# Unit 1's alpha turned on the matrix engine, wider filler products, last stores from one queue, and new orders in a GLA-then-MoE kernel

## The chip, the core and the metric

The kernel runs on one core of a Trainium2 chip. A core has a matrix engine (TensorE, PE in the profile; its weight loads are PEld), a vector engine (VectorE, DVE), an activation engine (ScalarE, ACT), GpSimd (POOL) and SyncE (SP). Each runs its own list of instructions in order, and they wait for one another through semaphores. Transfers between memory and the on-chip SBUF are issued by an engine's queue (here SP's and ACT's) and carried out by 16 DMA engines. TensorE writes into PSUM banks, which VectorE and ScalarE read. The metric is the device time of one execution in microseconds, lower being better.

## What is computed

First a gated linear attention, per batch and head a running 48x48 state; then an MLP on its output, whose nonlinearity is h - tanh(h).

```python
for t in range(S):                       # B,H,S,D = 4, 8, 768, 48
    state = alpha[:, :, t, :, None] * state + np.einsum('bhd,bhe->bhde', k[:, :, t], v[:, :, t])
    y[:, :, t] = np.einsum('bhd,bhde->bhe', q[:, :, t], state)
x = y.transpose(0, 2, 1, 3).reshape(B * S, H * D)      # 3072 x 384
h = x @ w_in                                           # w_in 384 x 2048
out = (h - np.tanh(h)) @ w_out                         # w_out 2048 x 384
```

The inputs q, k, v, alpha are float32; w_in and w_out are float64 in memory and are read as 64-bit integers and turned into float32 on the chip.

## The kernel before

The sequence is cut into 12 **units** of 256 tokens (two chunks of 128). The function `fast` does all of it; `general` is a slow form for inputs outside the range of the fast one, in a conditional at the end (line 1511) that is skipped when `ok` is 1.

For each unit the attention part (`gla`, from line 653) loads alpha, k, q and v, makes their transposes (aT, kT, qT: head dimension on partitions), makes prefix and suffix products of alpha by scans (`U`, `ends`, `W`), multiplies them into k and q (`kU`, `qW`), and then for each chunk computes masked scores, the output y and the new state on TensorE. In the first two units, which stand at the start of the program, transposes can be made by TensorE: `TURNED` (line 472) says for which of alpha, k, q (0, 1, 2). For such a tensor `load` (line 585) fetches a `rough` tile in natural layout with runs of 2 x 48 floats, 384 bytes, in two halves (line 604), `turn` (line 700) multiplies 32 blocks of 64x64 with the identity (line 718), and `place` or `times` copies the result out of PSUM. Otherwise `load` fetches runs of 8 x 48 floats, 1,536 bytes, onto 2 x 32 partitions (line 608), ScalarE copies a part (`widen`, line 684) and VectorE transposes blocks of 32x32 (`flip`, line 690). Unit 0's transfers are halved between SP's queue and ACT's.

The MLP of a unit has 8 **steps**. `first u:s` multiplies x by two column blocks of w_in into a PSUM bank (line 1243); ScalarE squares (`square`, `quad`), VectorE forms the cubic tail (`cube`, `shrunk`); `second u:s` multiplies by w_out and accumulates (line 1323). Units 0 and 1 do this plainly; units 2 to 11 use a scheme with 7 instead of 8 block products for w_out (line 1345; `combine` makes the combinations of w_out beforehand, `sums` those of g), and units 6 to 11 another one for w_in. x of a unit from 1 on is rearranged between partitions by six small DMAs on SP (`moves`, line 1145) before its first step. The first of all steps, `first_a 0:0` and `first 0:0`, is halved by chunk.

The weights come in 16 **pieces** (in0 to in7, out0 to out7), at the start of the program. `fetch` (line 560) has `load_weight` (line 38) issue the DMAs of a piece, six for w_in and one for w_out, into one of four `raw` tiles; `read` is the part of `round_weight` on ScalarE (lines 86, 87) and the second part, on VectorE (lines 89, 90), writes the float32 weights. Later `reload` fetches the pieces once more for a range check (`look`).

All this is issued in an order written out by hand: each piece of work is a named task with an engine, a cost, a due rank, the tasks it follows and a latency (`add`, line 386). `Planner.STEPS` holds the order of all tasks as steps between task numbers, made beforehand from these costs; `order` only checks it, works out start times, and puts filler products (`spin`, line 1425: identity times identity, 128x128) into the gaps of TensorE before the first y. Since each engine works in order, a task that waits holds up all that comes behind it on its engine. SP's queue is one of these engines: a load that waits for its tile holds the next fetch.

At the end, `store` of a unit scales and adds up four PSUM banks and issues four DMAs, those of the last unit two on ACT and two on SP (lines 1415 and 1418). After the last task each engine takes a branch over its part of `general`.

Of the kernel before, what the change touches and what calls it, by code (L numbers as in the profile page):

```python
# [8 lines left out]
FP32 = mybir.dt.float32  # L9
I32 = mybir.dt.int32  # L10
I64 = mybir.dt.int64
# [5 lines left out]
P = 128  # L17
HP = 64
CU = 2
WN = 768  # L20
# [17 lines left out]
def load_weight(nc, pool, rows, both=False, **kw):  # L38

    raw = pool.tile([P, WN], I64 if rows[0][2].dtype != FP32 else FP32, name="raw", **kw)  # L40
    for at, js, src in rows:
        (nc.scalar if both and at.start % HP == 0 and at.start else nc.sync).dma_start(  # L42
            out=raw[at].rearrange("p (j n) -> p j n", n=src.shape[-1])[:, js], in_=src)
    return raw
# [89 lines left out]
def general(tc, q, k, v, alpha, moe_w_in, moe_w_out, out, w_in, w_out, ident, pad_rows):  # L134
# [10 lines left out]
    with ExitStack() as ctx:  # L145
        with tc.tile_pool(name="g_raw", bufs=1) as raw_pool:
            for s in range(FT // 2):
                for what, dst in (("in", w_in[:, :, 2 * s * P:2 * (s + 1) * P]), ("out", w_out[:, 2 * s:2 * s + 2, :])):
                    raw = load_weight(nc, raw_pool, weight_parts(moe_w_in, moe_w_out, pad_rows, what, s))
                    round_any_weight(nc, raw_pool, raw, dst)  # L150
# [34 lines left out]
        for u in range(B * UPB):  # L185
# [3 lines left out]
            for c in range(CU):  # L189
                t0 = i * TU + c * P  # L190

                def rows(x):
                    return x[b, :, t0:t0 + P, :].rearrange("h p d -> p h d")
                for t, x in zip(nat, (alpha, k, q)):
                    nc.sync.dma_start(out=t[:, c, :, 0:D], in_=rows(x))
                nc.sync.dma_start(out=vt[:, c], in_=rows(v))
# [119 lines left out]
            for c in range(CU):  # L316
                ob = one.tile([P, d_model], FP32, name="g_ob")
                A.copy(ob, o[c])
                nc.sync.dma_start(out=out_r[u * CU + c], in_=ob)


class Planner:
# [6 lines left out]
        "90 1 1 2 -1 2 -95 100 -3 9 -10 7 11 -7 27 -30 6 -1 -4 27 -34 -97 98 18 16 -32 11 -4 10 17 -33 17 -117 135 -17 -117 139 -14 -15 8 -10 12 6 14 -28 9 "  # L329
        "-118 124 -8 -6 9 -121 127 13 -18 -117 127 -9 -122 2 506 -501 126 376 -369 3 -8 -132 512 -5 -505 5 501 -370 4 367 4 6 -376 -133 504 -509 -2 507 15 -517 "  # L330
        "-2 7 502 -384 386 -378 372 -378 383 4 -504 -7 2 133 377 5 -380 -134 520 -513 -5 513 3 -383 -132 503 4 -500 -5 131 375 -369 -9 393 -5 -515 2 5 509 -382 "
        "-11 -120 518 -390 -121 500 7 -11 5 -506 513 -383 2 -124 510 -385 -132 521 -395 -124 125 389 -506 123 -128 -2 504 11 -384 -128 7 -5 519 -392 387 -513 "
        "128 -126 502 -377 387 5 -516 512 6 -10 5 -384 388 -391 393 -517 512 -384 -2 379 -504 159 361 -3 -385 24 -28 398 -402 397 -388 390 -1 -384 -4 384 9 "
        "-367 364 4 -398 395 -381 -15 400 2 -396 1 21 -18 394 -3 -369 -21 394 5 -20 17 -346 345 -394 396 -375 -31 401 8 2 -379 -5 386 -6 -344 -57 54 350 -375 "
        "-24 22 382 -401 22 5 -29 27 26 356 -9 4 -401 23 -18 398 -1 2 -401 404 -388 390 -10 -353 -42 -3 5 405 -3 -406 408 -382 -6 383 -376 -4 27 360 -557 172 "
        "-171 174 383 -366 -39 -1 24 1 1 -176 152 27 378 2 -1 2 2 -561 180 -179 559 -384 386 -385 387 -557 556 3 -373 376 -4 -343 -27 381 -6 2 -1 -348 -42 386 "
        "-385 395 -4 -394 400 2 -7 4 -351 357 -16 -377 389 11 -370 364 -389 33 358 -12 11 6 -395 2 397 -388 385 -5 6 5 -17 -380 387 -364 370 -395 406 -598 589 "
        "-399 402 -591 574 19 5 4 -10 7 -404 -1 400 11 -413 4 404 -5 -602 204 409 2 -1 -606 611 -397 -15 -25 23 19 -43 -172 579 32 -412 416 -623 182 30 -2 397 "
        "2 12 -394 368 -387 44 -41 409 -18 -348 -26 -219 618 -398 -219 224 381 -384 385 -360 366 -12 -380 398 -368 357 13 -1 -394 -2 398 3 -10 8 -631 641 -7 "
        "-422 -202 203 422 -427 31 -15 424 -10 -627 625 6 -411 21 372 25 -6 1 -7 16 -3 6 -17 12 -26 38 -6 -12 -388 401 -12 13 -424 -223 659 -7 -651 655 -36 "  # L340
        "-396 436 -32 12 13 1 -12 -417 423 1 13 -1 -26 -633 240 -39 23 22 -46 441 -640 201 451 2 -7 13 1 -436 1 437 -391 -29 -242 240 30 401 -8 -433 -229 244 "
        "422 -13 18 -7 -396 -20 2 410 -415 29 389 9 -396 -30 -19 446 -401 -25 418 12 -3 -449 442 -416 -21 445 10 -457 450 -452 454 -1 3 -433 -248 251 429 11 -9 "
        "-430 -251 684 -18 20 -1 6 2 -1 3 -443 435 -20 31 -429 -40 459 -434 1 5 13 432 -6 2 -700 699 -398 -31 442 -7 -704 708 -434 398 40 -413 -71 77 -30 -24 "
        "-22 451 -403 415 13 1 -12 -414 -24 444 13 1 -13 -398 415 -445 -272 258 42 386 -432 -1 3 462 -459 -258 276 445 -28 -419 31 420 -20 8 6 -12 -428 435 -14 "
        "26 -8 -717 726 -450 431 20 -8 -718 282 438 -7 14 1 -7 9 -8 -721 277 451 -450 -277 729 2 -1 -452 455 -1 2 2 -440 -17 -24 1 44 -43 486 -6 -456 1 457 -1 "
        "2 -442 437 9 -416 420 -3 1 -419 424 -464 -286 746 -773 767 -739 756 -9 3 -419 420 29 -28 12 -435 424 -453 457 2 -19 25 -7 -431 440 -1 -5 -7 17 -470 "
        "-300 1 758 -477 489 -470 2 3 466 -800 801 7 -448 -51 466 14 -459 -22 501 -6 23 -16 -28 -469 514 -513 497 -478 2 -305 310 -8 496 -16 -22 5 34 -33 17 "
        "-782 771 12 -503 519 -15 -11 27 1 -16 17 -16 28 -11 -15 -22 21 17 -15 26 -9 -16 18 24 -16 -11 -31 59 -26 10 -816 808 25 -16 -43 -470 530 -16 17 -16 17 "
        "-531 515 17 -16 17 -16 28 -11 -49 61 -28 -32 33 16 12 -27 43 -15 -61 49 28 -15 -61 33 29 -13 28 -14 15 -28 1 13 -12 27 -63 64 -15 -48 49 28 -13 -13 -1 "
        "15 13 1 -78 65 14 -78 79 -14 -571 556 30 -11 -3 -15 16 14 -570 -39 -1 26 585 -587 3 517 -542 610 -67 -503 571 -67 76 -592 593 -8 -1 -567 24 553 -77 78 "  # L350
        "-62 34 29 -62 -514 577 -28 -546 575 14 -13 -581 517 -533 -4 538 64 -555 506 -532 594 18 -30 -49 62 18 -79 49 -48 51 -606 616 -601 619 -63 46 -13 14 "
        "-46 63 -16 -594 611 -614 598 -577 578 16 -50 -14 49 -48 31 33 -15 -35 63 -26 14 -32 45 -63 51 -592 605 -63 34 -33 -574 637 -62 49 28 -26 -35 62 -44 29 "
        "-10 -601 565 -605 623 -17 46 -45 -609 669 -14 -45 60 -646 647 -15 16 -32 -615 648 -16 -609 626 -32 44 -11 -17 -32 61 -43 -17 49 12 -29 1 -32 1 60 -11 "
        "-17 29 14 -27 14 -46 17 43 -13 -12 -1 27 -13 -12 26 1 -62 48 15 -62 -626 627 47 15 -13 -1 15 -13 -672 686 -13 14 2 8 -680 -39 24 635 -636 -24 661 50 "
        "10 -7 24 -712 -24 42 678 -60 77 -76 60 17 -16 -45 34 12 16 -61 -638 700 -16 17 -670 654 -12 29 -672 656 17 -714 727 -29 -700 702 15 -16 17 -700 712 -8 "
        "-70 1 78 -63 52 12 -63 -671 21 684 -33 63 -684 -46 745 -44 30 -63 -649 727 -62 48 -711 726 -749 735 -17 18 14 -704 -26 700 31 -64 50 15 -64 34 -33 49 "
        "-735 763 -26 -1 -35 63 -748 734 15 -14 15 -64 36 -717 682 49 -48 35 28 -14 28 -61 -694 729 -760 759 -33 47 -11 12 -13 14 12 1 -61 49 13 -61 62 15 -76 "
        "62 -764 750 29 -14 -13 28 -14 -15 30 -780 752 29 -64 18 47 -64 48 17 -30 31 -17 2 26 -10 -66 52 -51 48 46 -18 -26 -34 50 -796 825 -18 -60 61 -10 28 "
        "-17 -61 62 -61 48 30 -799 783 -805 822 -16 -13 30 1 -17 18 -49 32 -803 821 -16 2 -18 15 18 9 -813 -15 -26 776 -733 812 -78 70 -69 -732 733 -778 26 829 "
        "-61 -793 30 825 -28 -33 -772 834 -61 34 28 -61 48 14 -815 816 -831 832 -14 15 -50 61 -846 786 51 -50 -782 834 -51 48 -833 844 18 -27 10 -44 -803 865 "  # L360
        "-45 28 -44 45 -10 27 -16 -45 -786 832 -45 61 -15 16 -15 16 -846 2 845 1 -17 -33 -799 850 -17 28 -26 -35 34 28 17 -883 855 -50 79 -17 -61 53 26 -63 34 "
        "12 18 -63 17 17 12 -28 46 -63 46 -45 63 -30 13 -45 63 -17 18 -903 886 -864 882 -17 28 -42 -850 832 33 45 -44 -33 -841 901 -900 918 -77 48 12 -59 60 "
        "-11 28 -16 -45 35 -3 -31 -856 901 -44 60 -915 856 13 31 -13 29 -15 -31 47 1 -16 17 -30 14 -900 2 900 15 -16 17 -15 17 8 -950 944 -54 51 -50 35 25 -59 "
# [1179 lines left out]
```

## Time and profile before

| | |
|---|---|
| median of 3 runs | 563.54 us (562.07, 563.95, 563.54) |
| the profiled execution | 560.73 us |
| its span, first to last instruction | 558.9 us |
| granted clock of TensorE | 0.996 |
| TensorE from 60 to 550 us | busy 490.00 of 490 us |
| VectorE, ScalarE from 60 to 550 us | busy 417.15 and 314.45 us |
| turning one tensor of a unit on TensorE | 32 products in 64 rows, 1.16 us |
| `flip` of alpha, unit 1 | 4 transposes, 2.06 us |
| `widen` of alpha, unit 1 | 2 copies, 1.26 us |
| conversion of a piece | 2.1 us on ScalarE, 0.56 and 0.96 us on VectorE |

A row of such a table is read with its place: a busy time says how long an engine worked in a stretch, not whether the end of the kernel depended on it. The page gives the shares of the whole span; the windows give them by stretch; the chain of waits gives, followed back from the end, what released each piece of work; the timeline gives the instructions of an engine in order, with the idle time before each in brackets and the instruction that ended it. Times in these views count from the span's start. Durations of neighbouring products overlap, so the time of one is read from start to start.

### The profile page before, as it was taken

How to read it: one execution, taken by the hardware profiler on the slowest of the kernel's cores; microseconds unless marked ns; L12 is line 12 of the kernel's file. 1: busy time of each engine (PE TensorE's matmuls, PEld its weight loads, DVE VectorE, ACT ScalarE, POOL GpSimd, SP SyncE). 2: the span in 40 equal slices, each digit the busy share in tenths (PEclk: the TensorE clock that was granted, in tenths of full speed). 3: DMA queues.
4: the chain of work that ended last, by engine and by line, in shares of the span. 5: the costliest groups of instructions: out<-in, count | busy, mean ns of one | idle time of the engine just before them, and what ended most of it. 6: DMA issues, size and time to landing. Idle time of an engine off the chain costs nothing.

```text
span 558.9 us, 14579 instructions
## 1 busy us (share of the span) xinstructions
PE 545.1 (98%) x6003; PEld 496.8 (89%) x6003; DVE 469.3 (84%) x855; ACT 358.4 (64%) x723; POOL 4.9 (1%) x23
## 2 busy tenths in 40 slices
PE   7889999999999999999999999999999999999995
PEld 7777767778899999899999999999999999999994
DVE  7879989989999598896898789999899986756663
ACT  2699987637856749774687747647754654555550
POOL 3000000000000000000000000000000000000000
PEclk9999999999999999999999999999999999999998
DMA  9999764143284363663541021130020000100001
GB/s 214 223 261 253 242 120 143 30 91 117 57 182 110 86 164 79 161 152 86 138 155 57 29 63 33 57 74 22 28 64 5 29 8 3 32 6 0 30 2 35
DMA packets 59468, 50.88 MB, mean 91 GB/s; under 512 B 34528, under 2 KB 49152, under 8 KB 59392
## 3 DMA queue, kind: packets, MB, share of 16 engines
q1 hardware_dynamic: 56304, 48.58, 34.3%
q10 hardware_dynamic: 3088, 1.28, 0.9%
q8 instruction: 49, 0.80, 0.6%
q14 instruction: 27, 0.22, 0.1%
HBM read 44.04 MB, written 4.72 MB: 87 GB/s over the span
## 4 chain that ended last, share of the span: by engine, by line
PE 94%; DVE 1%; SPq 1%; issue 1%; DMA 1%; ACT 0%; POOL 0%; ACTq 0%; DVEq 0%; POOLq 0%
PE o L1345 32%; PE h L1243 23%; PE h L1254 14%; PE o L1323 7%; PE h L1275 7%; PE h L976 4%; PE sc L949 2%; PE sc L1122 1%; PE sc L956 1%; PE sc L976 1%; SPq L42 1%; DMA raw<-in_moe_w_in_dram 1%; PE spin L1429 1%; SPq L593 1%; DVE w_in L90 1%
## 5 line engine op out<-in xcount | busy, mean ns | idle before, releaser
L1243 PE MATMUL h<-xT,w_in 128*128 128x256 f32 (+1 forms) x588 | 131.6, 377 | 3.2 <-DVE w_in L90 3.2
L1243 PEld LDWEIGHTS h<-xT,w_in 128*128 128x128 f32 x588 | 108.1, 190 | 19.9 <-DVE w_in L90 4.2
L1345 PE MATMUL o<-b,e 128*128 128x192 f32 x480 | 93.3, 326 | 0.0
L1345 PEld LDWEIGHTS o<-b,e 128*128 128x128 f32 x480 | 79.1, 190 | 0.2
L1345 PE MATMUL o<-w_out,e 128*128 128x192 f32 x320 | 78.6, 328 | 0.0
L1299 DVE SCALAR_TENSOR_TENSOR g<-z,w 128x512 f32<-128x512 f32 x96 | 65.3, 684 | 12.8 <-ACT z L1290 5.7
L1345 PE MATMUL o<-b,g 128*128 128x192 f32 x320 | 68.9, 326 | 0.0
L1290 ACT ACTIVATE z<-u 128x512 f32<-128x512 f32 x96 | 60.2, 629 | 7.0 <-DVE g L1299 5.5
L1345 PEld LDWEIGHTS o<-w_out,e 128*128 128x128 f32 x320 | 55.0, 190 | 1.2
L1267 ACT COPY u<-h 128x128 f32<-128x128 f32 x96 | 24.6, 265 | 48.4 <-PE h L1254 47.5
L1254 PE MATMUL h<-xT,w_out 128*128 128x128 f32 x288 | 54.9, 275 | 0.0
L1254 PE MATMUL h<-xT,w_in 128*128 128x128 f32 x288 | 54.4, 277 | 0.0
L1280 DVE TENSOR_TENSOR w<-h,u 128x512 f32<-128x512 f32 x48 | 33.1, 690 | 25.3 <-PE h L1275 24.6
L1345 PEld LDWEIGHTS o<-b,g 128*128 128x128 f32 x320 | 53.8, 190 | 0.1
L1286 ACT ACTIVATE u<-w 128x512 f32<-128x512 f32 x48 | 30.3, 631 | 36.7 <-DVE w L1280 36.6
L1305 ACT ACTIVATE big<-u 128x1024 f32<-128x1024 f32 x48 | 50.6, 1054 | 0.4
L1254 PEld LDWEIGHTS h<-xT,w_in 128*128 128x128 f32 x288 | 47.9, 190 | 1.8
L1275 PE MATMUL h<-xT,w_in 128*128 128x256 f32 x192 | 49.2, 380 | 0.0
L1286 ACT ACTIVATE u<-h 128x512 f32<-128x512 f32 x48 | 28.4, 591 | 28.6 <-PE h L1243 28.4
L1312 DVE TENSOR_TENSOR e<-g 128x384 f32<-128x384 f32 x80 | 44.2, 552 | 2.8 <-PE o L1345 0.6
L1254 PEld LDWEIGHTS h<-xT,w_out 128*128 128x128 f32 x288 | 45.3, 191 | 0.4
L1323 PE MATMUL o<-w_out,g 128*128 128x384 f32 x128 | 43.4, 489 | 0.0
(167 smaller groups left out, 959.7 us busy)
## 6 DMA issues: line engine op xcount, KB each, us to landing
raw<-in_moe_w_out_dram SPq DMA_DIRECT2D x16, 768.0 KB, 6.1
raw<-in_moe_w_in_dram SPq DMA_DIRECT2D x16, 288.0 KB, 5.1
raw<-in_moe_w_in_dram SPq DMA_DIRECT2D x47, 96.0 KB, 5.0
vt<-in_v_dram SPq DMA_DIRECT2D x23, 192.0 KB, 3.6
ar<-in_alpha_dram SPq DMA_DIRECT2D x22, 192.0 KB, 3.9
kr<-in_k_dram SPq DMA_DIRECT2D x20, 192.0 KB, 3.1
qr<-in_q_dram SPq DMA_DIRECT2D x20, 192.0 KB, 3.2
raw<-in_moe_w_in_dram SPq DMA_DIRECT2D x15, 192.0 KB, 5.4
```

The source lines that it names most:

```text
L976: return T.matmul(to[rows], lhsT=lhsT, rhs=rhs, start=start, stop=last, skip_group_check=True)
L1243: T.matmul(h[:, a, to], lhsT=w_in[:, j, f * P:(f + 1) * P], rhs=xT[u][:, j, to], start=(j == 0), stop=(j == KT - 1))
L1254: T.matmul(m["h", s][:, to], lhsT=left[n][:, s], rhs=right[u][n], start=start, stop=True, skip_group_check=True)
L1275: T.matmul(m["h", s][:, 2 * a:2 * a + 2].rearrange("p i t -> p (i t)"), lhsT=wi[:, KT - 1, s, a], rhs=xT[u][:, KT - 1, :], start=False, st ...
L1280: V.tensor_add(m["w", s], m["h", s].rearrange("p i t -> p (i t)"), m["u", s])
L1286: A.activation(m["u", s], m["h", s], AF.Square, scale=W_SCALE ** -1.5)
L1290: A.activation(m["z", s], m["u", s], AF.Square, bias=QB, scale=QA * W_SCALE)
L1299: V.scalar_tensor_tensor(out=g.rearrange("p a c t -> p (a c t)"), in0=m["z", s], scalar=QK, in1=m["w", s], op0=ALU.add, op1=ALU.mult)
L1305: A.activation(big, m["us", s // 2].rearrange("p s t -> p (s t)"), AF.Relu, bias=-U_FAST, scale=W_SCALE, accum_out=over[:, n:n + 1])
L1312: V.tensor_sub(e[:, 0:3, :], x[:, 3:4].to_broadcast([P, 3, P]), x[:, 0:3])
L1323: T.matmul(m["o"][c], lhsT=g[:, a, c, :], rhs=w_out[:, f, :], start=(f == 0), stop=(f == FT - 1))
L1345: T.matmul(o[n][:, i], lhsT=g_, rhs=w_, start=(s_ == 0 and (n, i) in ((0, 0), (1, 0), (2, 1), (3, 0))), stop=(s_ == FS - 1), skip_group_ch ...
```

## The change

Five things are changed.

- `TURNED` has alpha of unit 1 too: it is loaded as a rough tile, turned by TensorE into a double PSUM bank of its own time (`early`), and copied by ScalarE and VectorE. Its turn comes after unit 0's qW; that of q comes after these copies.
- The filler has a second, longer product, 128x512 (the tile `after` is its moving side), used in gaps that are long enough. In the gap before the first task only short ones are used, counted with 2 instead of 1.75 lengths.
- The first piece of w_in is no longer halved between the queues (`BOTH_QUEUES` is 0), and the code for it is rewritten; SP issues its six parts.
- The last unit's stores are issued by SP alone. In `general` all DMAs are issued by ScalarE, so that SP has none there.
- Costs and latencies of loads, fetches and reads in the plan are changed, and the written order of all tasks on all engines is a new one.

In the new order TensorE does, after the turns of unit 0: back 0.0, update 0.0, scores 0.0, back 0.1, turn aT 1, update 0.1, scores 0.1, turn qT 1, y 0.0, carried 0.1, y 0.1, first_a 0:0, turn kT 1, first 0:0, first 0:1, back 1, scores 1.0, first 0:2, y 1.0, first 0:3, second 0:0, scores 1.1, first 0:4, second 0:1, y 1.1. Before it did: back 0.0, scores 0.0, update 0.0, turn qT 1, back 0.1, scores 0.1, y 0.0, update 0.1, carried 0.1, y 0.1, turn kT 1, first_a 0:0, first 0:0, first 0:1, back 1, first 0:2, first 0:3, second 0:0, scores 1.0, first 0:4, second 0:1, first 0:5, scores 1.1, y 1.0. SP does, after unit 0's loads: aT, kT, qT of unit 1, in0, in1, v of unit 1, in2, in3; before: in0, qT, aT, kT, v of unit 1, in1, in2, in3. From in2 on the fetches have the same order, up to out6.

```diff
-def load_weight(nc, pool, rows, both=False, **kw):
+def load_weight(nc, pool, rows, raw=None, of=None, of_all=False, **kw):
-    raw = pool.tile([P, WN], I64 if rows[0][2].dtype != FP32 else FP32, name="raw", **kw)
+    raw = raw or pool.tile([P, WN], I64 if rows[0][2].dtype != FP32 else FP32, name="raw", **kw)
     for at, js, src in rows:
-        (nc.scalar if both and at.start % HP == 0 and at.start else nc.sync).dma_start(
+        if of is not None and of != (at.start >= HP):
+            continue
+        (nc.scalar if of or of_all else nc.sync).dma_start(
             out=raw[at].rearrange("p (j n) -> p j n", n=src.shape[-1])[:, js], in_=src)
...
-                    nc.sync.dma_start(out=t[:, c, :, 0:D], in_=rows(x))
-                nc.sync.dma_start(out=vt[:, c], in_=rows(v))
+                    nc.scalar.dma_start(out=t[:, c, :, 0:D], in_=rows(x))
+                nc.scalar.dma_start(out=vt[:, c], in_=rows(v))
...
-                filled += [(free, -1, do, None)] * int(gap / (1.75 * us) if free == self.begin.get(engine) else gap / us - 1 if gap > 2 * us else 0)
+                first = free == self.begin.get(engine)
+                n = 0 if first else max(0, int((gap - us) / (4 * us)))
+                filled += [(free, -1, longer, None)] * n
+                gap -= 4 * n * us
+                filled += [(free, -1, do, None)] * int(gap / (2 * us) if first else gap / us - 1 if gap > 2 * us else 0)
...
-    BOTH_QUEUES = 1
+    BOTH_QUEUES = 0
...
-        TURNED = ((0, 1, 2), (1, 2))
+        TURNED = ((0, 1, 2), (0, 1, 2))
...
+                    elif what == 0 and u > 0:
+                        if c == 0:
+                            early = two_banks()
+                        t = early[:, c]
...
-                go("turn aT", "PE", 1.5 if u == 0 else 1.0, 0, ["load aT", later and "masked 0.0"], lambda: turn(0))
+                go("turn aT", "PE", 1.5 if u == 0 else 1.0, 0, ["load aT"] + [later and f"qW{x} 0" for x in "ab"], lambda: turn(0))
...
-                go("turn qT", "PE", 1.0, 2, ["load qT"] + [later and f"qW{x} 0" for x in "ab"], lambda: turn(2))
+                go("turn qT", "PE", 1.0, 2, ["load qT"] + [later and f"aT{x} {u}" for x in "ab"], lambda: turn(2))
...
-                    (A if u == NU - 1 and c == 0 else nc.sync).dma_start(out=half[1 - c], in_=cross[:, c, :])
...
-                    (A if u == NU - 1 and c == 0 else nc.sync).dma_start(out=half[c], in_=same[:, c, :])
+                for t, to in ((cross, 1), (same, 0)):
+                    for c in range(CU):
+                        n = abs(to - c)
+                        nc.sync.dma_start(out=out_r[u * CU + c][:, n * NH:(n + 1) * NH], in_=t[:, c, :])
...
-                spun.append(ps_o.tile([P, P], FP32, name="spin", tag="o2"))
-            T.matmul(spun[0], lhsT=ident, rhs=ident, start=True, stop=True)
-        plan.filler = "PE", "y 0.0", 0.24, spin
+                spun.append(ps_o.tile([P, 4 * P], FP32, name="spin", tag="o2"))
+            T.matmul(spun[0][:, 0:by.shape[-1]], lhsT=ident, rhs=by, start=True, stop=True)
+        plan.filler = "PE", "y 0.0", 0.24, spin, lambda: spin(after[:, 0:4 * P])
```

Left out are the lines of `STEPS`, the costs (for instance `fetch` of a piece of w_in from 3.2 to 4.0, of w_out from 2.9 to 2.2, `read` from 1.9 to 2.1), the rewritten `fetch` and the two changes of `general`'s weight load and store.

## The prediction

> **What bounds the kernel now.** I read the page from the top, then the windows, the waits, the chain, and at last the timeline of both ends. The page says that TensorE is the bound, and that only the first slices are not full:
>
> ```profile
> span 558.9 us, 14579 instructions
> PE 545.1 (98%) x6003; PEld 496.8 (89%) x6003; DVE 469.3 (84%) x855; ACT 358.4 (64%) x723; POOL 4.9 (1%) x23
> PE   7889999999999999999999999999999999999995
> DMA  9999764143284363663541021130020000100001
> ```
>
> The windows say where it lacks work and who else is full (columns: stretch, length, busy us of PE, PEld, DVE, ACT, POOL, then clock, DMA share, GB/s):
>
> ```profile
> 0.00:20.00 20.00, 16.27 (x372) 14.82 (x373) 16.15 (x35) 9.19 (x17) 4.93 (x23) 1.00 0.97 217
> 20.00:40.00 20.00, 16.75 (x208) 14.08 (x207) 15.35 (x22) 14.31 (x22) 0.00 (x0) 1.00 1.01 252
> 40.00:60.00 20.00, 20.00 (x276) 14.85 (x278) 18.62 (x36) 19.95 (x30) 0.00 (x0) 1.00 0.96 260
> ```
>
> From 40 to 545 us PE is full in every window, and its waits between 60 and 550 us list nothing. So the end is set by three things: when PE becomes full, what it must do, and the tail after its last product at 550.2. How it becomes full stands in the chain (start, length, what):
>
> ```profile
> 26.18 0.97 DVE w_in L90
> ...
> 27.20 2.73 PE h L1243 x22
> ...
> 30.04 0.97 DVE w_in L90
> ...
> 31.06 2.42 PE h L1243 x10
> ...
> 36.90 0.97 DVE w_in L90
> ...
> 37.91 2.86 PE h L1243 x12
> ```
>
> Three times PE stands before a conversion of w_in: first_a 0:0 began at 25.21 with two rows and went on at 27.20 (1.7 lost), 29.97 to 31.06 (0.9), 36.7 to 37.91 (1.2). The first stop is telling: piece in0 was converted by 16.43, so first_a waited for **in1**, which it doesn't read. And two of these conversions themselves waited for PE ("0.92 <-PE h L1243", "1.32 <-PE h L1243" in the timeline). The pieces of w_in are strided, and their extents overlap; so products and conversions of different pieces wait for each other in the order in which they are written. That makes a ping-pong: product, conversion of 0.97, product, with PE idle unless other PE work stands between.
>
> **The change, the start.** Unit 1's alpha loses two ACT copies (0.62 each) and four DVE transposes (18.21 to 20.13, 2.06 in sum). It gains 32 products on PE (64 rows; turn qT 1, the same shape: 16.46 to 17.55, **1.09**) and one copy each on ACT (0.59) and DVE (0.69). PE pays 1.09; DVE wins 1.4.
>
> The orders matter more. Up to 9.86 (the ends of unit 0) nothing moves: the turn of alpha waits for its load either way. Then DVE now does kUa, Wa, kUb, qWa, least, Wb, decay, qWb: by the rows of before 0.6, 1.15, 0.6, 0.6, 0.1, 1.2, 0.3, 0.6, so qWb ends at **15.0** (before 14.7, but then came in0, 1.7, ahead of the mask). qWb frees the bank that turn aT 1 needs. From there PE has an unbroken run, lengths from its timeline between 15.86 and 25.21: turn aT 1 1.09, update 0.64, scores 1.08, turn qT 1 1.09, y 0.0 1.37, carried 1.36, y 0.1 1.57: 8.2, to **23.2**. DVE keeps ahead: mask 16.2, aTb 16.85, U 1 (2.3) 19.15, mask 0.1 (1.3) 20.4, needed at 21.6. first_a now starts at 23.2, not at 25.2 (27.2), since it is written before in1's conversion.
>
> Next on PE: first_a 1.35, turn kT 1 1.09, first 0:0 1.35, first 0:1 2.59, back 1 0.77, scores 1.0 1.07, first 0:2 2.59, y 1.0 1.0, first 0:3 2.6, second 0:0 2.58: 17.0, to 40.2. Each conversion has a turn, back and scores, or y on PE beside it (1.09, 1.84, 1.0 against 0.97). What stays late: W 1 (2.3) stands ahead of in1 on DVE, so first 0:0 waits some 0.4; scores 1.0 needs the copies behind back 1 (0.95 on ACT, less 0.45 of products before them), 0.5; 0.2 each for the edges of in2 and in3. That makes **41.5**. Before, second 0:0 ended at 43.34 without scores 1.0 (1.07) and y 1.0 (1.01), which came later: 45.4 for the same work. Gain **3.9**, the turn of 1.09 paid.
>
> SP's queue: three loads of unit 1 go ahead of in0 and in1, and one of v behind them. From in2 on the bytes ahead are the same (5.5 MB up to in2; read at 27.5 before). load qT 1 needs a cleared tile, and its memset now stands on DVE behind kUa, at 10.5; behind it SP holds in0 and in1. Before, SP also stood until 10.01, so at most 1 us of an idle queue is added: in1 at some 23, in2 28.5, in3 32.4. ACT wants them at 22.5, 28.7, 32.5, so this costs nothing yet; two more us would be 1.5 on the end. in0 is needed at 23, lands by 19 and takes 2.1 on ACT and about 1 on DVE.
>
> A rule against the change: the Trainium skill, DMA: Bandwidth & Descriptors, Specifications, wants 512 B for line rate and speaks of read-modify-write below it; unit 1's alpha goes from runs of 1,536 B to 384 B. The row: the windows 2:4 and 4:6, when only such runs of 384 B move, give 222 and 323 GB/s; 20:22 and 22:24, weights in runs of 2,048 B, give 201 and 224. By the row its 384 KB cost 1.4 us, as before; if the rule cost half the rate, 1.4 more ahead of in0 (an estimate). I take the row, it is the same transfer.
>
> **Spins.** Five instead of seven at first, then two of four times the width. Fourteen rows took 3.35 early (0.48 a product), 17 took 2.16 later (0.25). The Trainium skill, TensorE: Matmul & The Clock Gate, Part 1, says that full clock needs some 3.4 us of sustained work; five spins end at 3.7 and PE idles until 4.8, so the wide ones may meet the slow clock. By the warm row they and one short end at 10.3, before kUa (10.5): no cost. By the cold one at 12.3, so state 0.0 comes at 14.3 for decay at 13.9: 0.4. I take 0 and keep 0.4.
>
> **The tail.** ScalarE no longer issues the last stores; SP issues four (0.33 each): the last at 553.3 instead of 552.9, cost 0.4. What this buys stands at line 1511, the end of the conditional (operation, count: ns, when):
>
> ```profile
> L1511 SPq EVENT_SEMAPHORE  x8: 17/17/17, 557.0 to 557.5; - x8
> L1511 DVEq COMPARE_BRANCH  x1: 72/72/72, 552.3 to 552.3; - x1
> L1511 SPq COMPARE_BRANCH  x1: 45/45/45, 553.3 to 553.3; - x1
> L1511 ACTq COMPARE_BRANCH  x1: 54/54/54, 553.3 to 553.3; - x1
> L1511 DVEq EVENT_SEMAPHORE  x1: 21/21/21, 555.4 to 555.4; - x1
> L1511 ACTq EVENT_SEMAPHORE  x1: 17/17/17, 557.0 to 557.0; - x1
> ```
>
> Each engine that jumps over the general form stands 3.1 to 3.7 us; SP comes last, then walks its semaphores to 558.9, 1.9 more. The Trainium skill, Runtime: NRT & Kernel Launch, Instruction fetch mechanics, says that a branch out of the prefetched pages forces a fetch. All of the general form's DMAs leave SP, so its jump has nothing to cross. Then SP waits only for the last store: SP's stores land in 1.7 (median), ACT's last in 3.7, beside the fetches. From 553.3: 555.0 to 557.0, and 1.4 of the semaphores is left: 556.4 to 558.4. DVE (555.4) and ACT, free to jump at 550.7 and so there by 554.4, don't hold it. I take 557.3, near SP's own row: **-1.6**. Ends: -2.5, and +0.4 (the issue alone) if SP still stands.
>
> **Sum.** -3.9 - 1.6 = -5.5. 558.9 becomes 553.4; with the 1.83 outside the span (560.73 against 558.9) 555.2. The median shown, 563.54, lies 2.8 above the profiled run; the same difference there gives **558.0**.
>
> **Rivals.**
> 1. *Conversions hold PE.* ACT is busy 19.95 of 20 us between 40 and 60, reads of weights (1.9 each) among it. If they come no earlier, PE can move only into its present margin: in7 was converted at 60.8 and used at 63.6, 2.8. Against it: ACT idled 5.7 between 20 and 40, and loses 0.65. Time: 563.54 - 2.8 - 1.6 = 559.1.
> 2. *Slower: moves of a unit come late.* SP issues six transfers per unit (3.97 and 4.15 us, landing 2.1) when x and rest are done; first u:0 waits. For unit 2 SP began at 116.68, so they landed about 122.9, and PE came to first 2:0 at 124.55: margin 1.6. In the new order three combines (1.75 each) instead of two, a mask and a shrunk stand before rest 2.1 on DVE. One late combine eats the margin, two cost 1.9. The same pattern stands in ten units: three that lose 1.9 each eat the gain of 5.5, and with four (7.6) it is slower, 565.6. Against it: the order before had the same pattern and lost nothing.
> 3. *Half of it.* A few such stalls or waits of PE elsewhere after 70 us, 3 us in all: 561.0. For it: the order is new everywhere; against it: the listed waits after 60 us are none today.
> 4. *The tail doesn't do what it says* (SP still fetches, or the last store lands late beside fetches): 563.54 - 3.9 + 0.4 = 560.0.
>
> **Numbers.** Forecast 0.44 (own range 556.3 to 560), rival 1 0.13, rival 4 0.12, rival 3 0.14, rival 2 0.17. No change is within 0.3%, 1.7 us, about what this measurement can tell: 561.9 to 565.2. Half of rival 3 reaches it, 0.02 of rival 4 and 0.02 of rival 2: faster 0.74, same 0.11, slower 0.15. Range 555.3 to 564: below, the tail's end of -2.5 with 5.2 of the start (none of the 1.3 of waits); above, 0.4 of the clock and 1.4 of the rule on short runs lie within it, and it reaches through rival 3 into rival 2.
>
> **What would show it.** The right chain: first_a at 23 to 24 with all rows in one run; no stop of over 0.5 before w_in; second 0:0 over at 41 to 42; SP's jump without a gap, the span ending within 7.2 us of PE's last product (now 8.6). Wrong: waits of PE on xT or on moves after 70 us, on w_in at first 0:6 or 0:7, or SP still standing 3.7 us at the conditional.

## The result, and the profile after

| | before | after |
|---|---|---|
| median | 562.23 us (10 runs, 561.01 to 564.59) | 559.06 us (10 runs, 558.41 to 560.69) |
| the profiled execution | 560.73 | 559.02 |
| its span | 558.9 | 557.2 |
| mean granted clock, middle of the runs | 0.994 (77 runs of all comparisons below) | 0.998 (10 runs) |

The ratio is 0.9943 (95% interval 0.9926 to 0.996): the change makes the kernel 3.2 us faster. The two profiles differ by 1.7 only; that discrepancy turns out to be a part of the answer. The page of the changed kernel, from its top:

```profile
span 557.2 us, 14660 instructions
PE 546.2 (98%) x6045; PEld 496.0 (89%) x6045; DVE 462.3 (83%) x853; ACT 357.9 (64%) x722; POOL 4.9 (1%) x23
PE   8999999999999999999999999999999999999995
DMA  9899962144672483464550041211200000000001
```

TensorE's first three slices have turned from 7, 8, 8 to 8, 9, 9; the others show the same digits as before. The windows of the same kernel (stretch, length, busy us of PE, PEld, DVE, ACT, POOL, clock, DMA share, GB/s):

```profile
0.00:20.00 20.00, 17.66 (x440) 14.88 (x440) 16.18 (x33) 9.35 (x17) 4.93 (x23) 1.00 0.92 229
20.00:40.00 20.00, 19.13 (x315) 15.99 (x311) 18.40 (x32) 16.39 (x26) 0.00 (x0) 1.00 0.96 238
40.00:60.00 20.00, 20.00 (x196) 14.41 (x195) 16.88 (x29) 19.21 (x29) 0.00 (x0) 1.00 1.01 288
```

TensorE works 3.8 us more ahead of 40 us than before (36.8 against 33.0). Of this the new turn of alpha is 1.1, while the filler products (spins) take 6.1 instead of 7.6. Its timeline at the start of the MLP, w_in's products and the first of w_out:

```profile
23.09 1.60 PE L1258 MATMUL h<-xT,w_in 128*128 128x128 f32 x12
...
25.71 0.49 PE L1258 MATMUL h<-xT,w_in 128*128 128x128 f32 x2
26.89 3.97 PE L1258 MATMUL h<-xT,w_in 128*128 128x128 f32 x22 [0.69 <-DVE w_in L92]
...
32.98 2.86 PE L1258 MATMUL h<-xT,w_in 128*128 128x256 f32 x12
...
36.97 2.86 PE L1258 MATMUL h<-xT,w_in 128*128 128x256 f32 x12
39.67 2.74 PE L1338 MATMUL o<-w_out,g 128*128 128x384 f32 x8
```

first_a 0:0 stands at 23.09 in one run of 12 rows (before: two rows at 25.21, the rest at 27.20). One stop of 0.9 is left, at first 0:0, and second 0:0 ends at 42.4 (before: 43.3, with scores 1.0 and y 1.0 still to come).

And then 2 us are given back. The waits of TensorE between 40 and 552 us list nothing for the kernel before; after, they list (who, for whom: us in all, times, longest):

```profile
PE h L1258 <- ACT xT L1040: 0.7, 1, 0.7
PE h L991 <- DVE w L1295: 0.3, 1, 0.3
```

A list of waits leaves out a part of a stop, since the time of a product that is still running isn't idle. So I took every product's time from its start to the next start, less the median of its shape. Both traces can be compared so, since their counts of rows differ by just the 64 of the turn and the 22 fewer of spins. Before has no stop over 0.2 us behind 40. After has four: 0.89 at 175.5, 0.30 at 309.7, 0.51 at 354.6, 0.27 at 484.5, **1.97** in sum. The last twelve products begin at 548.55 instead of 549.99, 1.44 earlier; so the start was worth 1.44 + 1.97 = 3.4.

The tail is the third part. Line 1524 is the end of the conditional (operation, count: ns, when):

```profile
L1524 SPq EVENT_SEMAPHORE  x8: 17/17/17, 552.5 to 555.8; - x8
L1524 DVEq COMPARE_BRANCH  x1: 72/72/72, 550.9 to 550.9; - x1
L1524 SPq COMPARE_BRANCH  x1: 50/50/50, 552.3 to 552.3; - x1
L1524 DVEq EVENT_SEMAPHORE  x1: 21/21/21, 553.8 to 553.8; - x1
```

SP now passes its branch without a gap (552.3, then 552.5; before 553.3, then 557.0). But the semaphores behind it last until 555.8, since the store issued at 551.82 comes late: 15 of its 16 parts have landed by 554.16, the last one at 555.69. From the start of the last twelve products to the end of the span it is 8.65, before 8.91: 0.3 won.

### The profile page after: what moved, and what is told of

It is laid out like the page before. It is cut to its first block, busy times and chain, and to the rows that moved or that the text cites. A ratio compares the mean times of both kernels' runs of the same rounds, so it can differ in the third digit from the quotient of the medians.

```text
span 557.2 us, 14660 instructions
## 1 busy us (share of the span) xinstructions
PE 546.2 (98%) x6045; PEld 496.0 (89%) x6045; DVE 462.3 (83%) x853; ACT 357.9 (64%) x722; POOL 4.9 (1%) x23
## 4 chain that ended last, share of the span: by engine, by line
PE 91%; SPq 2%; DVE 2%; ACT 2%; DMA 1%; issue 1%; POOL 0%; DVEq 0%; POOLq 0%
PE o L1360 32%; PE h L1258 22%; PE h L1269 13%; PE o L1338 8%; PE h L1290 7%; PE h L991 3%; SPq L44 2%; PE sc L964 2%; DMA raw<-in_moe_w_in_dram 1%; PE sc L1137 1%; DVE same L1423 1%; PE sc L971 1%; PE sc L991 1%; DVE w L1295 1%; PE turned L733 1%
## 5 line engine op out<-in xcount | busy, mean ns | idle before, releaser
L1295 DVE TENSOR_TENSOR w<-h,u 128x512 f32<-128x512 f32 x48 | 33.0, 687 | 33.9 <-PE h L1290 33.8
L1269 PE MATMUL h<-xT,w_out 128*128 128x128 f32 x288 | 53.3, 275 | 0.0
L1327 DVE TENSOR_TENSOR e<-g 128x384 f32<-128x384 f32 x80 | 44.4, 555 | 2.6 <-PE o L1360 0.8
L1310 DVE TENSOR_TENSOR w<-h,u 128x512 f32<-128x512 f32 x48 | 32.8, 687 | 14.9 <-ACT u L1301 14.9
L1269 PEld LDWEIGHTS h<-xT,w_out 128*128 128x128 f32 x288 | 44.1, 192 | 0.1
```

The costliest lines, as they stand in the source:

```text
L1269: T.matmul(m["h", s][:, to], lhsT=left[n][:, s], rhs=right[u][n], start=start, stop=True, skip_group_check=True)
L1295: V.tensor_add(m["w", s], m["h", s].rearrange("p i t -> p (i t)"), m["u", s])
L1310: V.tensor_mul(m["w", s], m["h", s], m["u", s])
L1327: V.tensor_sub(e[:, 0:3, :], x[:, 3:4].to_broadcast([P, 3, P]), x[:, 0:3])
```

## The experiments

Each is shown with its edit, what it was expected to do, and its ratio to the kernel before in runs on the same chip; the changed kernel's is 0.9943, and 0.001 is 0.56 us.

### The tail: its edits alone, half of them, and no jump at all

`tail_alone` is the kernel before with this:

```diff
-    (A if u == NU - 1 and c == 0 else nc.sync).dma_start(...)   # last stores
+    nc.sync.dma_start(...)
-    nc.sync.dma_start(...)                                      # all of general's
+    nc.scalar.dma_start(...)
```

> The kernel before with the tail's edits alone: SyncE issues all last stores, ScalarE the general form's transfers. Theory A, from the trace after: SyncE's jump no longer stands, but its last store lands some 3.9 us after its issue, so the end moves by 0.3 only: ratio 0.9995 (0.999 to 1.000). Theory B, the prediction: SyncE was what ended the span and its store lands in 1.7: -1.6 us, ratio 0.997; it would also explain why the medians differ by 3.2 us where the two profiles differ by 1.7. Both expect SyncE to pass the conditional without a gap.

561.39 us, ratio 0.9998 (0.9985 to 1.0012), so the tail's edits won 0.8 us at most. A holds: no gain that can be measured, though SP passes the conditional without a gap (558.0, then 558.1). The part of the medians that the profiles don't show isn't the tail's. One pair of profiles can't size the tail at all: from the last twelve products to the end of the span it lasts 8.2 to 8.9 us in the four profiles here that have the tail of before, and 7.0 to 8.7 in the seven that have the changed one, so the 0.3 above lies within that spread.

`split_stores` is the changed kernel with the first of these two edits undone.

> The changed kernel with one edit of the tail undone: ScalarE again issues half of the last stores, the general form's transfers stay on ScalarE. Theory A (who issues matters little, the late landing sets the end): within 0.4 us, ratio 0.9995 to 1.0007; ScalarE, which now jumps only after its store, at 551.5, is back by 554.4 and is not last. Theory B (SyncE alone is what won the tail): 1.0 to 1.6 slower, ratio 1.002 to 1.003.

558.55, ratio 0.9949 (0.9929 to 0.9969). A again in the time, but not in one point: A had ScalarE back by 554.4 and not last, and the row of the conditional that comes last is now ScalarE's:

```profile
L1524 SPq EVENT_SEMAPHORE  x8: 17/17/17, 552.4 to 554.5; - x8
...
L1524 ACTq EVENT_SEMAPHORE  x1: 17/17/17, 555.2 to 555.2; - x1
```

ScalarE jumps at 552.2 and is there at 555.2; the stores have landed by 554.2.

`no_general` ends `tile_gla_recurrent__then__act_tanh_shrink_kernel` behind the call of `fast`; it leaves out the general form:

```diff
-    with tc.If(fine < 1):
-        general(tc, q, k, v, alpha, moe_w_in, moe_w_out, out, w_in, w_out, ident, pad_rows)
```

> The changed kernel without the conditional and the general form behind it (that part of the computation is left out; the inputs of the run never need it), so that no engine jumps. Theory A: the last store is held up by the instructions that the jumps fetch (its parts land between 553.4 and 554.2, one at 555.7, while fetches move until 554.8): now it lands within 2 us of its issue with all parts within 0.5, and the kernel is 1.7 to 2.5 us shorter, ratio 0.996. Theory B: the last of four stores in one queue lands late by itself: it still lands 3.5 to 4 us after its issue and the ratio is 0.999 to 1.000.

556.81, ratio 0.9914 (0.9897 to 0.9931): 1.6 us off the changed kernel by the ratios, 2.2 by the medians. A holds, and B is out. Its last store is issued at 551.68, and all its parts land between 553.21 and 553.37, 1.5 to 1.7 us later: SP's own figure, which the prediction took. TensorE's last twelve products begin at 548.4 (548.55 in the changed kernel); the tail is 6.0 instead of 8.65. So the jumps cost about 2 us even when SP's own costs nothing. The instructions that the engines fetch (16 KB and 8 KB transfers between 549.3 and 554.8 in the trace after) share the DMA engines with the last store, as the packets in the traces show. In the trace after, the last nine packets of the stores don't move until a 16 KB transfer of instructions (553.07 to 554.63) is over; in the trace before, nine packets of ScalarE's last store stand in the same way behind one of 554.12 to 555.57. This is so in eight of the thirteen profiles with jumps: there the last store lands 1.0 to 1.4 us after the end of that transfer, 2.9 to 3.9 after its issue. In the other five no packet of a store is left when that transfer ends, and the landing takes 2.2 to 2.5. The Trainium skill, Runtime: NRT & Kernel Launch, Instruction fetch mechanics, says that a taken branch out of the fetched pages costs a fetch to the engine that takes it; that a store of another queue pays too is what these runs add.

### The given-back time: stops of TensorE behind 42 us

At 175.5 the order has `scores 4.1`, which also holds unit 4's first output products, directly ahead of `first 3:3`; the latter wants the PSUM bank that ScalarE has still to copy (`x 4.0`). In the changed kernel's timeline first 3:3 begins with this row:

```profile
176.37 1.99 PE L1258 MATMUL h<-xT,w_in 128*128 128x256 f32 x8 [0.68 <-ACT xT L1040]
```

A first attempt, `hole_175`, added a table `MOVES` (task, behind which) to the order:

```diff
+    MOVES = (("second 2:7", "scores 4.1"), ("store 2", "second 2:7"),)
+        for name, behind in self.MOVES:
+            order.remove(names[name])
+            order.insert(order.index(names[behind]) + 1, names[name])
```

> The changed kernel with the largest stop of TensorE behind 42 us filled: second 2:7 and store 2 are moved behind scores 4.1, so that first 3:3 no longer follows at once on the products whose bank ScalarE has still to copy. Theory A (TensorE is the bound, every stop of it counts in full): the stop of 0.9 at 175.8 is gone and the kernel is 0.7 to 0.9 shorter, ratio 0.9985. Theory B (a stop is paid back: another engine sets the pace there, and TensorE stops later instead): ratio 0.9995 to 1.001 with a new stop behind 176.

559.87, ratio 0.9972 (0.9958 to 0.9986): slower than the changed kernel, and the stop grew from 0.89 to 1.35. I had built a new one: store 2 has a ScalarE part, which now stood ahead of `x 4.0` on that engine and waited for second 2:7. (In the profiled run of this kernel weights also landed late: stops of 2.0 in all between 50 and 63 us, where the edit reaches nothing.) Neither theory was tested by this. `holes` leaves ScalarE's order alone:

```diff
+    MOVES = (("second 2:7", "scores 4.1"), ("store 2", "state 4.1"), ("second_2 6:4", "first 6:7"),)
```

> The changed kernel with three tasks moved: second 2:7 behind scores 4.1, store 2 behind state 4.1 (the earlier attempt left store 2's ScalarE part ahead of x 4.0, which made it wait for second 2:7), second_2 6:4 behind first 6:7. Theory A (TensorE is the bound behind 42 us, each stop counts in full): the stops of 0.9 at 175 and 0.5 at 354 shrink by 0.9 and 0.3, the kernel is 0.9 to 1.2 shorter than the changed one, ratio 0.992 to 0.9928. Theory B (another engine sets the pace there): ratio 0.9937 to 0.995, with a stop in another place.

558.11, ratio 0.9926 (0.9901 to 0.9951), 0.95 under the changed kernel by the medians. The waits behind 40 us have lost their largest row; what is left of them, and TensorE's timeline where the stop was:

```profile
PE h L995 <- DVE w L1299: 0.3, 1, 0.3
```

```profile
175.24 1.14 PE L1364 MATMUL o<-b,e 128*128 128x192 f32 x6
176.22 5.34 PE L1262 MATMUL h<-xT,w_in 128*128 128x256 f32 x24
```

second 2:7 runs into first 3:3 and 3:4 without a break. The stop at 354 stayed (0.50), so its third move did nothing. A fits the medians, with the one stop of 0.89 for the 0.95, but the intervals of the two kernels overlap, and the traces show less. The profiled run of `holes` began second 0:0 0.47 later than that of the changed kernel and the last twelve products 0.07 earlier (548.48): 0.5 won on the way, after a new stop of 0.2 at 358.8. The other 0.9 by which its span is shorter lies in its tail, which the edit doesn't touch.

### The start: the turn, the extents, the spins

`turn_undone` is the changed kernel in its order, with `TURNED = ((0, 1, 2), (1, 2))`; `wide aT 1` stands behind `state 0.0`, `aT 1` where aTb 1 was, and the turn of q waits for qW.

> The changed kernel, in its order, with unit 1's alpha again widened by ScalarE and transposed by VectorE. Theory A, the prediction's (VectorE leads the start: 1.4 won on it for 1.09 paid on TensorE): VectorE's U 1 and W 1 come 1.4 later, in1's conversion behind them too, so TensorE's stop at first 0:0 grows from 0.9 to over 2; 1.0 to 1.6 slower, ratio to before 0.996 to 0.997. Theory B (VectorE has room there and TensorE's order alone is what the change won): the 1.09 us of products saved come off, ratio 0.9925 to 0.9935.

559.71, ratio 0.9957 (0.994 to 0.9973): 0.8 slower by the ratios, 0.65 by the medians, with an interval that overlaps the changed kernel's. B is out; A has the sign in these numbers, and half the size, which the noise allows to be nothing. Its timeline:

```profile
27.85 3.97 PE L1258 MATMUL h<-xT,w_in 128*128 128x128 f32 x22 [0.86 <-DVE w_in L92]
...
40.62 2.74 PE L1338 MATMUL o<-w_out,g 128*128 128x384 f32 x8
```

The stop at first 0:0 grew by 0.17 only, and second 0:0 begins 0.95 later than after. The profiles of other kernels with the changed start show it up to 0.7 later too, so between 0.3 and 0.95 of this is the turn's. (Its profiled run, at 560.78, was slow for this kernel, with further stops of 1.1 in all between 286 and 293 us, whose cause stays open.)

`apart_before` is the kernel before with another layout of w_in:

```diff
-    w_in = consts.tile([P, KT, d_ff], FP32, name="w_in")
+    w_in = consts.tile([P, FT // 2, KT, 2 * P], FP32, name="w_in")
...
-    dst = w_in[:, :, 2 * s * P:2 * (s + 1) * P]
+    dst = w_in[:, s]
-    lhsT=w_in[:, j, f * P:(f + 1) * P]
+    lhsT=w_in[:, f // 2, j, f % 2 * P:(f % 2 + 1) * P]
```

> The kernel before with w_in laid out piece by piece (128 x 8 x 3 x 256 instead of 128 x 3 x 2048), nothing else; the extents of its pieces no longer overlap. Theory A, the prediction's ping-pong: first_a 0:0 no longer waits for in1's conversion, nor conversions for products of other pieces; first_a and first 0:0 run in one, the stops of 1.7 and 0.9 go, that before first 0:2 or 0:3 (1.2) stays in part since in2 and in3 land when they land: 1.5 to 2.8 us faster, ratio 0.995 to 0.9973. Theory B (the conversions are late by themselves, behind VectorE's other work and the loads): no change, ratio 0.9993 to 1.0007, the same three stops.

560.18, ratio 0.9974 (0.9953 to 0.9995): 1.5 us, the low end of A. TensorE's timeline:

```profile
25.46 1.60 PE L1243 MATMUL h<-xT,w_in 128*128 128x128 f32 x12
27.40 4.20 PE L1243 MATMUL h<-xT,w_in 128*128 128x128 f32 x24 [0.33 <-ACT xT L1030]
...
33.02 2.86 PE L1243 MATMUL h<-xT,w_in 128*128 128x256 f32 x12 [0.66 <-DVE w L1295]
...
37.46 2.83 PE L1243 MATMUL h<-xT,w_in 128*128 128x256 f32 x12 [1.58 <-DVE w_in L90]
```

first_a runs in one, as the ping-pong theory wanted: it had waited for a piece that it doesn't read, and only because extents overlap. But of the three stops, 3.7 us in sum, 3.1 are still there (0.49, 0.82 and 1.75 from start to start). The largest stands before the conversion of in3, which is late by itself; the other two are listed behind ScalarE's xT and VectorE's w. The last twelve products begin 0.6 earlier than before (549.41), so the trace shows less than half of the 1.5. The ping-pong was real and the smaller half of the matter; what the changed order does besides is to put scores 1.0 and y 1.0 beside the late conversions.

`apart_after` is the same layout in the changed kernel.

> The changed kernel with w_in laid out piece by piece, as apart_before. Theory A (what is left of the start's stops is extents): the stop of 0.9 at first 0:0, which waits for in1 without reading it, goes, those of 0.3 stay; 0.6 to 1.0 shorter than the changed kernel, ratio 0.9927 to 0.9935. Theory B (the stop moves on to first 0:1, as conversions themselves are late): ratio 0.9937 to 0.995.

559.36, ratio 0.9958 (0.9942 to 0.9974). In its trace the stop at first 0:0 is gone, and second 0:0 begins 0.5 earlier (39.18); but its waits behind 40 us have a new row, one that nothing in the profile explains:

```profile
PE h L1258 <- ACT xT L1040: 0.7, 1, 0.7
PE o L1360 <- issue: 0.6, 1, 0.6
PE h L991 <- DVE w L1295: 0.3, 1, 0.3
```

Its twelve runs spread from 557.67 to 561.84. The start of the trace goes A's way, but the time is above what both theories put (its interval reaches into B's range, not into A's); the cause stays open.

`spins_old` is the changed kernel with the filler of before, `spins_new` the reverse:

```diff
-   filled += [(free, -1, do, None)] * int(gap / (1.75 * us) if free == self.begin.get(engine) else ...)
+   n = 0 if first else max(0, int((gap - us) / (4 * us)))
+   filled += [(free, -1, longer, None)] * n
+   gap -= 4 * n * us
+   filled += [(free, -1, do, None)] * int(gap / (2 * us) if first else ...)
```

> The changed kernel with the filler of before. Theory A (the spins hold the clock): mean granted clock 0.993 to 0.995 in most runs, half clock somewhere between 10 and 24 us, and 1.0 to 2.0 us slower than the changed kernel: ratio to before 0.9961 to 0.998. Theory B (spins are worth nothing): clock 0.997 to 0.999, ratio 0.9943 as the changed kernel.

> The kernel before with the changed filler alone (its planner then writes six short spins, three wide ones and four short ones). Theory A, new: most runs of the kernel before have a mean granted clock of 0.993 to 0.995, the run whose profile was shown 0.996, the changed kernel 0.996 to 0.999; so the filler of before lets TensorE's clock fall early in most of its runs, and the part of the gain that the two profiles don't show (3.2 between the medians, 1.7 between the profiles) is the spins'. Then this kernel has a clock of 0.997 or more and is 1.0 to 2.0 us faster, ratio 0.9965 to 0.998. Theory B, the prediction's: spins are worth 0 (-0.4 to +0.4), ratio 0.9993 to 1.0007, and the clock stays at 0.994.

559.45, ratio 0.9946 (0.9926 to 0.9965), and 561.78, ratio 0.9998 (0.998 to 1.0017). A falls in both: the filler is worth nothing that can be measured (each interval is some 1 us to either side), as the prediction had it, and the clock of `spins_old` stays at 0.996 to 1.0. What keeps the clock is in the order, not in the spins.

### The part that the profiles don't show

The mean clock of the kernel before was at most 0.996 in 68 of 77 runs; that of the changed kernel is 0.997 or more in 9 of 10. Part of that costs nothing: in both profiles the granted clock falls to half after TensorE's last product and stays there to the end of the span, 4.5 us in before, which is all that its 0.996 lacks, and 2.6 us in after. What costs time is half clock among the products. Three of the five profiles with the order of before have it ahead of 25 us (tail_alone, read_later, spins_new), and none of the nine with the changed order. The profile of `tail_alone`, a run with 0.988, shows where. TensorE's timeline in before, in tail_alone and in after, the row of spins and the one behind it:

```profile
8.04 2.16 PE L1429 MATMUL spin<-ident 128*128 128x128 f32 x17
11.89 1.61 PE L1429 MATMUL spin<-ident 128*128 128x128 f32 x13 [1.69 <-issue]
```

```profile
8.27 2.16 PE L1427 MATMUL spin<-ident 128*128 128x128 f32 x17
13.78 1.44 PE L1427 MATMUL spin<-ident 128*128 128x128 f32 x6 [3.35 <-issue]
```

```profile
7.99 1.98 PE L1442 MATMUL spin<-after,ident 128*128 128x512 f32 x4
9.81 0.38 PE L1442 MATMUL spin<-ident 128*128 128x128 f32 x2
10.32 0.60 PE L1050 MATMUL y<-ident,kT 112*128 112x112 f32 x4
```

In the kernel before TensorE stops **in the middle of fifteen equal products** (30 rows) that wait for nothing ("issue"). In four profiles with that start and filler (before, tail_alone, apart_before, read_later below) this comes behind the same row, the 447th of TensorE's products and weight loads, and ends 2.75 to 2.83 us after the start of a 16 KB transfer of the queue named "instruction": at 9.10, 10.95, 9.88 and 11.01 us, stops of 1.69, 3.35, 1.63 and 2.81. That points to the fetch of its next instructions, late by a different amount in each run; no run here moves that fetch alone. In `spins_old` the same row has a stop of 0.35, and goes on 2.4 us after its transfer began. The windows tell what follows, for tail_alone and before (the clock is the third figure from the end):

```profile
14.00:20.00 6.00, 6.00 (x35) 5.39 (x34) 3.13 (x5) 2.50 (x3) 0.00 (x0) 0.50 0.90 200
```

```profile
14.00:20.00 6.00, 5.53 (x132) 4.64 (x132) 5.42 (x11) 5.13 (x11) 0.00 (x0) 1.00 0.98 224
```

Behind a stop of 1.7 the clock stays full. Behind 3.35 it is half from 12.72 on for 10.24 us (tail_alone), behind 2.81 from 13.88 on for 3.41 us (read_later). (The Trainium skill, TensorE: Matmul & The Clock Gate, Part 1, has half clock follow a lack of recent work; the rows agree.) In tail_alone 35 rows run from 14 to 20 us instead of 132, and second 0:0 begins at 44.4 instead of 40.6. The profile that I had of the kernel before was of a run with a short stop: 560.73, where the median is 562.23.

The order before has a second gap of this sort. In the profile of spins_new the fetch costs at most 0.4, but ScalarE stands 2.55 us for in0's landing ahead of a copy that TensorE waits for, and the clock falls all the same:

```profile
14.00:16.00 2.00, 0.63 (x15) 0.44 (x15) 1.82 (x4) 1.62 (x3) 0.00 (x0) 1.00 1.11 241
16.00:18.00 2.00, 2.00 (x76) 1.91 (x71) 2.00 (x4) 1.52 (x3) 0.00 (x0) 0.54 1.06 220
```

It is half from 16.16 on for 3.41 us, behind a stop of 1.4 only, so the length of one stop doesn't decide it. In every trace the changes of the clock lie whole multiples of 3.41 us apart; by what the clock is set at these moments no run here shows.

`read_later` takes that second gap from the kernel before:

```diff
+    MOVES = (("read in0", "wide aT 1"), ("in0", "aT 1"),)
```

> The kernel before with two tasks moved in its order, nothing else: ScalarE's read of in0 goes behind wide aT 1 and VectorE's conversion of in0 behind aT 1. Theory A, new, from the traces: in the order before, ScalarE stands 2.5 to 3 us for in0's landing ahead of the copy (natural 0.0) that TensorE's update 0.0 waits for, TensorE has 0.6 to 1.5 of 2 us of work between 14 and 16, and in most runs its clock then falls to half for 3 to 10 us; the changed order reads in0 late, and that, not the spins, keeps the clock. Then: mean clock 0.997 or more in most runs, 0.8 to 2.0 us faster, ratio 0.9965 to 0.9985. Theory B (the clock falls for another reason, or what is won is lost at w_in's conversions): ratio 0.9993 to 1.001, clock 0.994.

561.78, ratio 0.9995 (0.9979 to 1.0012): A falls as it was put. The copy no longer waits for in0, but this profile has the other gap, at row 447, of 2.81 us, and half clock from 14 to 16. So each of these two kernels closes one gap, profits in none, and shows the other. That both closed together are worth the missing 1.5 us is argued from these traces, not shown by a run. It fits that the nine of the 77 runs of the kernel before with a mean clock of 0.997 or more have a median of 560.9, where that of all is 561.64. The changed order has neither gap, and its clock is steady.

### A version meant to beat both

`all_three` is the changed kernel with holes, the layout of w_in and split stores.

> A version meant to beat both: the changed kernel with holes, apart_after and split_stores together. If the gains add (1.0, 0.8 and 0.5): ratio 0.989 to 0.991. If the stops only move: 0.993 to 0.995.

557.69 (11 runs, 556.4 to 561.37), ratio 0.9931 (0.9909 to 0.9953). It has the lowest median of those that compute everything, and a spread that leaves it undecided against `holes` (0.9926), which is the simpler one, with five runs between 557.72 and 558.19. The ratio is the one expected if the stops only move, not if the gains add. Both intervals lie clear of 1, neither lies clear of the changed kernel's.

## Why the prediction was right, and where it was not

The forecast was 558.0 within 555.3 to 564, faster with 0.74; it is 559.06, 0.56% faster. But the sum behind it was -5.5 on the profiled execution, and that moved by 1.7. Point by point:

- *The bound* (TensorE full, so the end moves with the start of its work): right. When `holes` removed the largest stop behind 42 us, the median fell by its length (0.95 for 0.89), though the intervals overlap and its trace shows 0.5 ahead of the tail.
- *The start, -3.9*: -3.4 by the last products, -3.0 by the prediction's own measure, the end of second 0:0 (42.4 for 41.5, against 45.4). The steps came as put: turn aT 1 at 14.71 (15.0), first_a at 23.09 (23.2). Between first_a and the end of second 0:0 the waits were 1.45 in sum where I had 1.3 (0.9 at first 0:0 for 0.4, 0.3 each for natural 1 and in3). The mis-sized term is the products, 17.8 for 17.0: I took the lengths that they have in a long run of equal ones, and in the trace the first rows behind a change of kind take 0.1 to 0.25 more. The cause was half right: overlapping extents made the first stop, but without them the other conversions are late by themselves. Of the turn, 0.3 to 0.95 is shown where the sum gave VectorE 1.4. That the new orders won the rest is shown by elimination: with the turn undone the ratio is still 0.9957, with the old filler 0.9946, and tail and filler alone give 0.9998 each. The first piece of w_in on one queue instead of two was not tested apart.
- *Nothing lost behind 42 us*: this step failed. Rival 3 named stalls of up to 3 us; there were 1.97, nearly half of them one hole in the order, where products whose bank a copy must first clear are followed at once by those that want it. The sign "waits of PE on xT after 70 us" did appear, once, with 0.7 at that hole. No wait on rival 2's moves is listed.
- *The spins, 0*: right, in both directions, within 1 us. The wide ones ran at the warm rate (four rows in 1.98 us), and the short ones behind them ended at 10.2 for 10.3.
- *SP's queue and the short runs of alpha*: no loss seen. From 6 to 13 us, when the loads of unit 1 move, all transfers together make 285 GB/s (before 230), and in0 was read at 17.3.
- *The tail, -1.6*: -0.3 in the profile, nothing by `tail_alone`. SP's jump did lose its gap; the failed term is the landing of its last store, put at 1.7 by SP's median and measured 3.9 (2.2 to 3.9 in the other profiles with jumps), beside fetches of the other engines. The prediction had 3.7 as its other end, and the row of ACT's last store, taken in just that place, was the better one.
- *The step from profile to median*: I carried a constant 2.8 us (563.54 less 560.73) over to the changed kernel. It isn't constant: before's profiled run was one of its better ones, by 1.5 against its median, and the changed kernel's is at its median. This gain, which I put down to the fetch and the clock at 10 to 20 us (argued above, not shown by a run), was in no step of the prediction. It made up for nearly half of what the tail and the stops fell short: -5.5 + 0.5 + 2.0 + 1.3 - 1.5 = -3.2. That the time came within 1.1 us of the forecast is in part luck.
- *The range*: its lower end doesn't follow from its own terms; 563.54 less 2.5 and 5.2 is 555.8, not 555.3. Nothing hangs on it here.

## What to carry to other kernels

When TensorE is the bound and an order is rewritten, an early gain is worth what is left after the new order's own holes: list every start-to-start excess over 0.2 us in the new trace, and fill the place where a copy out of PSUM stands between two neighbours on TensorE. A profile is one run: before it is used as the base of a sum, compare its time with the spread of the runs: the one used here lay 1.5 us under its kernel's median. Compare its clock too, but by stretch, since a mean also counts the time behind the last product. And take a transfer's landing from the row that ran in the same surroundings, not from the median of its queue.

## What the runs showed of the hardware

- TensorE can stop in straight-line code, for its own instructions as the times suggest: 1.6 to 3.4 us at one fixed row in four profiles, while transfers fill the DMA engines (a share of 1.0 to 1.1 from 8 to 14 us in before and tail_alone). It goes on 2.75 to 2.83 us after a 16 KB transfer of instructions begins to move, 2.4 in `spins_old`.
- A stop of 1.7 us left the granted clock full; stops of 2.8, 3.35 and, in `spins_new`, 1.4 were followed by half clock, for 3.4, 10.2 and 3.4 us.
- An engine's jump slows transfers that are not its own: beside fetches the last store landed in 2.2 to 3.9 us, and in 1.7 without any, though the queue that issued it had nothing to fetch. In eight of thirteen profiles its last packets stood until a 16 KB fetch was over.
